# Block 0 of a fused attention and two-layer kernel: the third weight chunk's conversions placed behind the input's squares and its root, with 24 filler matmuls in place of 36

## The chip, the cores and the metric

The kernel runs on one core of a Trainium2 chip. The metric is device time in microseconds (us), the median of several runs. One more execution is recorded by the hardware profiler, and all rows of the trace come from that one.

## The reference

Attention over 4 batches, 8 heads, 576 positions of 64 numbers: the first four heads see a local window of 32 positions, the other four see every 32nd position. Its output, 2304 tokens of 512 numbers, goes through two gated layers with 1536 inner columns, the first behind a normalisation by the root of the mean square:

```
scores = where(mask, q @ k.T / 8, -1e9);  x = softmax(scores) @ v
rms = sqrt(mean(x * x) + 1e-6);  xn = x / rms * rms_g
y   = (silu(xn @ w_gate) * (xn @ w_val)) @ w_out
out = ((y @ w_a) * (y @ w_b)) @ w_out2
```

Every product keeps about single precision: both factors are split into a high part and a low part, and three matmuls (hi hi, hi lo, lo hi) are summed.

## The kernel before, in words

The 2304 tokens are worked through in 6 blocks of 384 (t = 0 to 5). In each block the attention's output gives four tiles of 128 x 384, the inputs 0 to 3. Inputs 0 and 1 come from the local heads, 2 and 3 from the strided ones. The first layer then runs over 12 chunks of 128 inner columns (fc). Per chunk PE makes a gate product g_ps and a value product v_ps of 12 matmuls each (`mm_in`, lines 485 to 488, `mm3`, 480 to 483), VectorE (DVE) multiplies g_ps by the reciprocal root `rinv` into sg (line 774), ScalarE (ACT) takes silu (776), DVE multiplies by v_ps (787), `split` makes the high part on ACT (506) and the low part (507), both called hl, and PE adds the 12 output matmuls (y) of the chunk before (`emit_y`, 595 to 603). The second layer follows after block 5. Three PSUM banks serve g_ps and v_ps in turn; in block 0 the product with sg is written over v_ps, so such a bank is held until hl is made.

Block 0 has more to do: the weights arrive as 64-bit words and are converted while it runs. A conversion (`conversion`, `words`, `parts`, lines 113 to 169) is one list of three steps: two activations on ACT (lines 137 and 142), an or-step on DVE (145); then the high part, a cast on ACT (150), and the low part, a subtraction on GpSimd, POOL (151). Gate and value weights of a chunk go together, 1024 columns (`convert1`, 543 to 550; chunk 0 in two halves), output weights alone, 512 columns (lines 789 to 793), and are then written out for the later blocks by a DMA on SP (793). SP also issues the loads (line 111).

The root's path in block 0: `xhl` (383 to 390) scales an input tile into its high part on ACT (387), squares it on ACT (432), and makes its low part on DVE (389). A matmul with a matrix of ones adds the squares of each of the four inputs (436). Two buffers hold squares, so the third square needs the first sum's matmul, the fourth the second's. `rinv` (446 to 450) is the square root on ACT (448) and the reciprocal on DVE (450). `keep_busy` (558 to 563) issues filler matmuls that nobody reads, 128 x 256 in bfloat16: 20 at the start (WARM) and 36 here, "id36" in STEPS0 (line 42), not before the last transpose of the inputs.

The order of instructions on each engine is chosen when the program is built, by a planner that has its own estimate of durations; once built, each engine runs its list in order. `behind` and `gate` (lines 496 to 502 and 581 to 587) bind that order: what is traced inside comes, on an engine, after the named instruction on the same engine. They add no wait between engines. `GATES` (line 45) lists for the chunks 0, 1, 2, 3 and from 4 on which instructions those are: "xhi" is the last scaled copy of an input (ACT), "sqrt" the root (ACT), "rec" the reciprocal (DVE), "snorm", "sqr" and "pvr" are steps of the strided attention on DVE, "pvm" one on POOL.

Of the kernel before, what the change touches and what calls it, by code (L numbers as in the profile page):

```python
# [14 lines left out]
AF = mybir.ActivationFunctionType  # L15
# [23 lines left out]
LOADS0 = "la0 lq ls0 cst la1 lb0 lvl1 lb1 lvl0 lv0"  # L39
STEPS0 = ("sqk00 sqk01 sqk02 qk0 qk1 qk2 smask0 lmax0 lexp0 smask1 lmax1 lexp1 smask2 ssub sexp "  # L40
          "lnorm0 snorm lmax2 lexp2 pt0 ptc0 lnorm1 sqrt_set pt1 ptc1 spv00 spv01 spv02 lnorm2 pt2 "
          "ptc2 pv0 pvc0 pv1 pvc1 xst0 xst1 xstc0 id36 xstc1 rms rinv")
WARM = 20

GATES = ["pvm snorm sqr",
         "norm pvm snorm sqr",
         "pvr snorm xhi",
         "snorm sqr sqrt xhi",
         "rec sexp snorm sqrt xhi"]

# [17 lines left out]
WLO = ["PPP", "PPP", "PPP", "PPP", "PPP", "PPP",  # L68
       "PPP", "PPP", "PPP", "PPP", "PPP", "PPD"]

LOW = ["AAA"] * NFC
# [6 lines left out]
def fused_kernel(ctx: ExitStack, tc: tile.TileContext, qtl, ktl, vl, qs, ks, vs, cst, w1, w2, out):  # L78
# [5 lines left out]
    nc = tc.nc  # L84

    def engine(c):
        return {"P": nc.gpsimd, "D": nc.vector}[c]
# [17 lines left out]
    def gv_slot(dtype, name):  # L105
        return wgt.tile([128, 2, 2, DM], dtype, tag="gv", name=name, bufs=NFC)
# [18 lines left out]
    def words(third, z, low="A"):  # L125

        third = third.rearrange("p a n -> p (a n)")
        raw = third.rearrange("p (n t) -> p n t", t=2)
        y = raw[:, :, 1].bitcast(F32)

        def first():
            nc.scalar.activation(y, y, AF.Prelu, scale=-2.0 ** -80, alpha=-2.0 ** -32)
            if low == "D":
                nc.vector.tensor_scalar(z(), raw[:, :, 0], 29, None, op0=ALU.logical_shift_right)
            else:  # L140
                half = third.bitcast(U16).rearrange("p (n t) -> p n t", t=4)[:, :, 1]
                nc.scalar.activation(z(), half, AF.Copy, scale=2.0 ** -13, bias=2.0 ** -14 - 0.5)

        def second():
            nc.vector.scalar_tensor_tensor(z(), raw[:, :, 1], 3, z(), op0=ALU.logical_shift_left, op1=ALU.bitwise_or)

        return [first, second]

    def parts(x, hi, lo, lo_eng):
        nc.scalar.copy(hi, x)  # L150
        lo_eng.tensor_tensor(lo, x, hi.bitcast(F32), op=ALU.subtract)  # L151

    def conversion(third, ready, pool, lo_eng, low, out=False):

        st = {}
        n = ready.shape[1] // 2

        def z():
            if not st:
                st["z"] = pool.tile([128, (1 if out else 2) * DM], U32, tag=f"cz{out}", name="cz", bufs=NCZ[out])  # L160
            return st["z"][:, :n * DM]

        def last():
            x = z().bitcast(F32).rearrange("p (a n) -> p a n", a=n)
            hl = ready.rearrange("p (a s) n -> p a s n", s=2)
            parts(x, hl[:, :, 0], hl[:, :, 1], lo_eng)

        return words(third, z, low=low) + [last]

    def run(steps):  # L170
        for f in steps:
            f()
# [14 lines left out]
    def attention(t, pool, psum, banks):  # L187
# [4 lines left out]
        st = {}  # L192
        steps = {}

        def bank():
            return psum.tile([128, 512], F32, tag=next(banks), name="att")

        def piece(tag, name, bufs):
            return pool.tile([128, NTB], F32, tag=tag, name=name, bufs=bufs)
# [228 lines left out]
        def sq(i):  # L428
            def f():
                q_t = st["sq", i] = piece("sq", "sq", 2)  # L430
                src = st["ops" if i < 2 else "xps", i % 2][:, :NTB]
                nc.scalar.activation(q_t, src, AF.Square)
                if t == 0:
                    if i == 0:
                        st["rps"] = bank()
                    nc.tensor.matmul(st["rps"][:, :NTB], ones, q_t, start=i == 0, stop=i == 3)
                elif i:
                    engine(SQA[t]).tensor_tensor(q_t, q_t, st["sq", i - 1], op=ALU.add)
            return f
# [54 lines left out]
    silu, silu_gate = [], []  # L494

    @contextmanager
    def behind(instructions):

        with ExitStack() as e:
            for i in instructions:  # L500
                e.enter_context(tc.issue_after(i))
            yield
# [21 lines left out]
    pool = apool.enter_context(tc.tile_pool(name="early", bufs=1))  # L524
# [18 lines left out]
    def convert1(fc):  # L543
        t = gv[fc] = gv_slot(F32R, "gv")
        two = [raw.pop((fc, k)) for k in range(2)]
        if fc in FUSEDW:
            both, ready = gvraw[fc], t.rearrange("p k a n -> p (k a) n")
            run(conversion(both.rearrange("p k a n -> p (k a) n"), ready, pool, engine(WLO[fc][0]), LOW[fc][0]))
        else:
            run(zipped(*(conversion(two[k], t[:, k], pool, engine(WLO[fc][k]), LOW[fc][k]) for k in range(2))))  # L550

# [16 lines left out]
    s0 = attention(0, pool, psum, itertools.cycle(["att", "y0", "y1", "y2", "y3"]))  # L568
# [12 lines left out]
    @contextmanager  # L581
    def gate(fc):

        with behind(silu[:1] if fc > 4 else []), ExitStack() as e:
            for key in GATES[min(fc, len(GATES) - 1)].split():
                e.enter_context(tc.issue_after(s0["st"][key].ins))
            yield

    with gate(0):
        convert1(0)  # L590
# [22 lines left out]
    def load_wo(t, fc):  # L613
        wt = wo[t, fc] = wo_tile()
        nc.sync.dma_start(wt.rearrange("p a n -> p (a n)").bitcast(F32), wod[fc])
# [126 lines left out]
    for t in range(NB):  # L742
        if t == 1:
            apool.close()
            pool = apool.enter_context(tc.tile_pool(name="attn", bufs=1))
        if t == NB - 1:
            apool.close()
            cpool.close()
            pool = p2.enter_context(tc.tile_pool(name="forms", bufs=1, reuse_waits="tile"))
            early = [f for k in (4, 5, 0, 1, 2, 3) for f in convert_forms(k, k < 4)]  # L750
        nxt = attention(t + 1, pool, psum, itertools.cycle(["att"])) if t + 1 < NB else None
        if t == 0:
            exps(nxt)
        x = [xt[t, cc] for cc in range(NCC)]
        for fc in range(NFC):
            if t > 0 and fc == 0:
                load_wo(t, 0)
            g_ps = psum.tile([128, 512], F32, tag="gv", name="g_ps", bufs=3)
            mm_in(g_ps[:, :NTB], gv[fc], 0, x)
            v_ps = psum.tile([128, 512], F32, tag="gv", name="v_ps", bufs=3)  # L760
            mm_in(v_ps[:, :NTB], gv[fc], 1, x)
            if t == 0 and fc + 1 < NFC:
                with gate(fc + 1):
                    convert1(fc + 1)
                if fc + 2 == NFC:
                    load_late([(NFC - 2, 2), (NFC - 1, 2)])
            if t == NB - 1:
                slab[fc] = wgt.tile([128, 4 * DM], F32 if fc in (0, 1, 11) else F32R, tag="gv", name="slab", bufs=NFC)
                with behind(made):
                    run(early[len(early) * fc // NFC:len(early) * (fc + 1) // NFC])  # L770
                    for k in [k for k in x0 if k <= fc]:
                        run(x0.pop(k))
            sg = tmp("sg")
            nc.vector.tensor_tensor(sg, g_ps[:, :NTB], ri[t], op=ALU.mult)  # L774
            with behind(silu_gate):
                silu.append(nc.scalar.activation(sg, sg, AF.Silu).ins)  # L776
            silu_gate[:] = []
            if fc == 1 and t > 0:
                evac_y(t - 1)
            if nxt is not None:  # L780
                attention_slot(nxt, fc)
            if prev is not None:
                emit_y(*prev)
            if t > 0 and fc + 1 < NFC:
                load_wo(t, fc + 1)
            h = tmp("h") if t else v_ps[:, :NTB]
            made[:] = [nc.vector.tensor_tensor(h, sg, v_ps[:, :NTB], op=ALU.mult).ins]
            hl[t, fc] = split(h, engine(HLO0[fc] if t == 0 else HLO[t]))
            if t == 0:
                wt = wo[0, fc] = wo_tile()  # L790
                with gate(fc + 1), behind(silu[:1] if fc > 1 else []):
                    run(conversion(raw.pop((fc, 2)), wt, pool, engine(WLO[fc][2]), LOW[fc][2], True))
                nc.sync.dma_start(wod[fc], wt.rearrange("p a n -> p (a n)").bitcast(F32))
                if fc % 2 and units:
                    load_units(1)
            prev = (t, fc)
# [140 lines left out]
    steps = [(ps, g, p) for ps in (range(0, 3), range(3, 6)) for g in range(NB // 2) for p in ps]  # L937
# [3 lines left out]
    for i, (ps, g, p) in enumerate(steps):  # L941
# [12 lines left out]
        a, pa = products(g, 2 * p)  # L954
# [82 lines left out]
```

## Time and profile before

| | us |
|---|---|
| median of 3 runs | 964.89 |
| lowest and highest of them | 964.42, 965.96 |
| the profiled execution | 967.4 |
| its span in the trace | 965.6 |
| mean granted PE clock in it | 0.985 of full speed |

The span is what the trace shows from the first to the last instruction; the profiled execution's own time has 1.8 us more around it, and it is 2.51 us above the median. All positions below are us from the span's start. In a row of a timeline the columns are start, duration, engine, line, operation, output<-input, shape, count, and in brackets the idle time of the engine before it and who ended it. PEld is PE's loading of weights. A row with a count covers that many instructions, merged.

### The profile page before, as it was taken

Reading aid. Unit: us, or ns where it says so; the run is one execution under the profiler, and the core shown is the slowest. Engines: PE = TensorE matmul, PEld = TensorE weight load, DVE = VectorE, ACT = ScalarE, POOL = GpSimd, SP = SyncE. Lnnn points to the kernel's source line nnn. Section 1 sums busy time; section 2 is a strip of 40 time slices with the busy share of each in tenths; the row PEclk is TensorE's granted clock in tenths of the full one; section 3 lists DMA queues with packets and bytes.
Section 4 is the critical chain, followed back from the end, with each engine's and each line's share of the span. In section 5 each row is a group of like instructions: output and inputs, shape, how many; then the busy total and the mean of one; then the engine's idle time right before and its main releaser. Section 6 shows DMA issues by size and latency. Waiting matters only on the chain.

```text
span 965.6 us, 14099 instructions
## 1 busy us (share of the span) xinstructions
PE 937.1 (97%) x5318; PEld 888.2 (92%) x5318; DVE 621.5 (64%) x900; ACT 425.3 (44%) x795; POOL 539.5 (56%) x407
## 2 busy tenths in 40 slices
PE   5998999999999999999999899999999999999998
PEld 4898999999999999999999898899999998999996
DVE  5658858658819895986666378658655655564534
ACT  5988646344433434434555455436425422122110
POOL 3567946558649677878479545655724423123211
PEclk6899999999999999999999999999999999999999
DMA  9974286537535563532788884996993974754701
GB/s 342 408 262 151 89 288 218 151 96 225 165 104 161 161 204 102 185 105 87 284 324 306 329 306 166 402 415 247 385 373 114 345 274 165 284 205 168 267 2 66
DMA packets 57363, 215.55 MB, mean 223 GB/s; under 512 B 5968, under 2 KB 14544, under 8 KB 51664
## 3 DMA queue, kind: packets, MB, share of 16 engines
q1 hardware_dynamic: 57296, 214.66, 61.3%
q8 instruction: 42, 0.69, 0.3%
q14 instruction: 25, 0.20, 0.1%
HBM read 172.17 MB, written 42.47 MB: 222 GB/s over the span
## 4 chain that ended last, share of the span: by engine, by line
PE 65%; DMA 11%; DVE 7%; POOL 7%; ACT 4%; issue 4%; SPq 0%; DVEq 0%; ACTq 0%; POOLq 0%
PE o L916 5%; PE o L918 5%; PE o L917 5%; DMA raw<-in_w 4%; POOL prod L248 4%; PE Y L862 4%; PE Y L861 4%; PE Y L860 4%; DMA gv_raw<-in_w 3%; PE y L482 3%; PE y L481 3%; PE g_ps L483 3%; PE y L483 3%; PE g_ps L482 3%; PE g_ps L481 3%
## 5 line engine op out<-in xcount | busy, mean ns | idle before, releaser
L151 POOL TENSOR_TENSOR hl<-c,hl 128x384 fp32r<-128x384 f32 x72 | 77.9, 1082 | 181.0 <-ACT hl L150 174.4
L248 POOL TENSOR_TENSOR prod<-kv_t,qs_t 128x512 f32<-128x512 f32 (+12 forms) x57 | 108.3, 1921 | 15.3 <-DMA kv_t<-in_ks 8.2
L481 PE MATMUL v_ps<-xx,gv 128*128 128x384 f32 x288 | 97.7, 339 | 1.9 <-DVE sg L774 1.8
L482 PE MATMUL y<-hl,wo 128*128 128x384 f32 x288 | 98.1, 341 | 1.1 <-POOL hl L507 1.1
L281 POOL TENSOR_TENSOR prod<-kv_t,S_t 128x512 f32<-128x512 f32 (+12 forms) x57 | 86.2, 1526 | 21.1 <-issue 7.1
L482 PE MATMUL v_ps<-xx,gv 128*128 128x384 f32 x288 | 97.9, 340 | 0.0
L483 PE MATMUL v_ps<-xx,gv 128*128 128x384 f32 x288 | 97.8, 340 | 0.0
L481 PE MATMUL g_ps<-xx,gv 128*128 128x384 f32 x288 | 97.5, 339 | 0.0
L483 PE MATMUL g_ps<-xx,gv 128*128 128x384 f32 x288 | 97.3, 338 | 0.0
L482 PE MATMUL g_ps<-xx,gv 128*128 128x384 f32 x288 | 96.9, 337 | 0.0
L867 DVE TENSOR_TENSOR c<-c,Y 128x384 f32<-128x384 f32 x108 | 59.0, 551 | 58.8 <-PE Y L862 53.5
L507 POOL TENSOR_TENSOR hl<-h,hl 128x384 fp32r<-128x384 f32 x60 | 64.1, 1069 | 58.4 <-ACT hl L506 57.3
L483 PE MATMUL y<-hl,wo 128*128 128x384 f32 x288 | 95.0, 338 | 0.0
L284 DVE TENSOR_REDUCE xs_t<-prod 128x64 f32<-128x448 f32 (+17 forms) x57 | 85.7, 1521 | 9.7 <-POOL prod L281 9.5
L481 PE MATMUL y<-hl,wo 128*128 128x384 f32 x288 | 85.0, 343 | 7.0 <-ACT hl L506 5.4
L916 PE MATMUL o<-slab,hl 128*128 128x512 f32 x216 | 84.7, 393 | 1.8 <-DVE slab L925 1.3
L917 PE MATMUL o<-slab,hl 128*128 128x512 f32 x216 | 84.5, 392 | 0.0
L918 PE MATMUL o<-slab,hl 128*128 128x512 f32 x216 | 83.2, 394 | 0.0
L150 ACT CAST hl<-c 128x384 fp32r<-128x384 f32 x72 | 37.0, 514 | 93.8 <-DVE c L897 93.5
L776 ACT ACTIVATE sg<-sg 128x384 f32<-128x384 f32 x72 | 38.0, 528 | 86.4 <-DVE sg L774 86.0
L862 PE MATMUL Y<-slab,form 128*128 128x384 f32 x216 | 73.0, 338 | 0.0
L861 PE MATMUL Y<-slab,form 128*128 128x384 f32 x216 | 73.0, 338 | 0.0
(137 smaller groups left out, 2491.4 us busy)
## 6 DMA issues: line engine op xcount, KB each, us to landing
form<-formd SPq DMA_DIRECT2D x32, 1792.0 KB, 10.7
wo<-wod SPq DMA_DIRECT2D x60, 512.0 KB, 3.8
raw<-in_w SPq DMA_DIRECT2D x40, 512.0 KB, 7.3
gv_raw<-in_w SPq DMA_DIRECT2D x32, 512.0 KB, 10.2
formd<-form SPq DMA_DIRECT2D x6, 1792.0 KB, 7.5
formd<-forms SPq DMA_DIRECT2D x6, 1792.0 KB, 12.8
slab<-x2d SPq DMA_DIRECT2D x24, 384.0 KB, 4.0
wod<-wo SPq DMA_DIRECT2D x12, 512.0 KB, 3.4
```

Source lines behind the costliest of these rows:

```text
L151: lo_eng.tensor_tensor(lo, x, hi.bitcast(F32), op=ALU.subtract)
L248: nc.gpsimd.tensor_tensor(pr, st["ks", g][:, :, :n, :], st["qs"][:, heads(g), mm:mm + 1, :].to_broadcast([128, G, n, D]), op=ALU.mult)
L281: st["pvm"] = nc.gpsimd.tensor_tensor(pr, st["vs", g][:, :, :n, :], st["S"][:, heads(g), mm, :n, None].to_broadcast([128, G, n, D]), op=AL ...
L284: st["pvr"] = nc.vector.tensor_reduce(st["xs"][:, mm, heads(g), :], pr.rearrange("p g n d -> p g d n"), axis=X, op=ALU.add)
L481: nc.tensor.matmul(out_ps, w_hi, x_hi, start=start, stop=False)
L482: nc.tensor.matmul(out_ps, w_hi, x_lo, start=False, stop=False)
L483: nc.tensor.matmul(out_ps, w_lo, x_hi, start=False, stop=stop)
L861: nc.tensor.matmul(bank(n), hi, x[p][:, 1, c], start=False, stop=False, skip_group_check=not begins)
L862: nc.tensor.matmul(bank(n), lo, x[p][:, 0, c], start=False, stop=c == 1, skip_group_check=not begins)
L916: nc.tensor.matmul(o, h[:, 0, cols], w[0], start=n == 0, stop=False)
L917: nc.tensor.matmul(o, h[:, 0, cols], w[1], start=False, stop=False)
L918: nc.tensor.matmul(o, h[:, 1, cols], w[0], start=False, stop=n == len(chunks) - 1)
```

## The change

In `GATES`, the entry for chunk 2 gets "square" (the last square, on ACT) and "xlo" (the last low part of an input, on DVE). In `convert1` the last step of chunk 2's conversion (cast and low part) is put behind the root. The output weights of chunk 1, which used the entry of chunk 2, use that of chunk 3, whose member on ACT is the root. The fillers are 24.

```diff
-          "ptc2 pv0 pvc0 pv1 pvc1 xst0 xst1 xstc0 id36 xstc1 rms rinv")
+          "ptc2 pv0 pvc0 pv1 pvc1 xst0 xst1 xstc0 id24 xstc1 rms rinv")
...
-         "pvr snorm xhi",
+         "pvr snorm xhi square xlo",
...
-                nc.scalar.activation(q_t, src, AF.Square)
+                st["square"] = nc.scalar.activation(q_t, src, AF.Square)
...
-            run(conversion(both.rearrange("p k a n -> p (k a) n"), ready, pool, engine(WLO[fc][0]), LOW[fc][0]))
+            steps = conversion(both.rearrange("p k a n -> p (k a) n"), ready, pool, engine(WLO[fc][0]), LOW[fc][0])
+            run(steps[:-1])
+            with behind([s0["st"]["sqrt"].ins] if fc == 2 else []):
+                run(steps[-1:])
...
-                with gate(fc + 1), behind(silu[:1] if fc > 1 else []):
+                with gate(3 if fc == 1 else fc + 1), behind(silu[:1] if fc > 1 else []):
```

## Rows read from the trace of the kernel before

**Rows 1.** The page: engine, busy us, share of the span, instructions.
```profile
PE 937.1 (97%) x5318; PEld 888.2 (92%) x5318; DVE 621.5 (64%) x900; ACT 425.3 (44%) x795; POOL 539.5 (56%) x407
```
**Rows 2.** Stretches of the head: busy us of each engine, granted PE clock, DMA share, GB/s.
```profile
29.00:30.00 1.00, 1.00 (x10) 0.85 (x9) 0.67 (x2) 0.83 (x1) 0.00 (x0) 0.87 1.03 397
...
33.70:49.95 16.25, 14.62 (x79) 13.13 (x76) 10.82 (x13) 15.92 (x23) 6.51 (x3) 1.00 1.03 408
49.95:51.80 1.85, 0.02 (x1) 0.02 (x1) 0.10 (x2) 1.85 (x4) 1.37 (x1) 1.00 1.06 415
51.80:58.00 6.20, 6.20 (x26) 6.20 (x27) 3.40 (x5) 6.20 (x10) 2.25 (x2) 0.72 1.04 400
...
86.30:94.20 7.90, 4.90 (x19) 4.35 (x20) 7.84 (x13) 7.87 (x14) 2.84 (x2) 0.78 0.68 239
```
**Rows 3.** Timeline of PE, fillers to the first gate matmul.
```profile
27.87 2.59 PE L563 MATMUL idle<-ones 128*128 128x256 bf16 x16
...
30.95 0.93 PE L563 MATMUL idle<-ones 128*128 128x256 bf16 x7
31.71 0.81 PE L436 MATMUL att<-sq,ones 128*128 128x384 f32 x2
32.36 1.58 PE L563 MATMUL idle<-ones 128*128 128x256 bf16 x13
33.70 0.42 PE L481 MATMUL g_ps<-xx,gv 128*128 128x384 f32 x1
```
**Rows 4.** Timeline of ACT, chunk 2's first activation to the cast of hl 0.
```profile
31.90 1.16 ACT L137 ACTIVATE gv_raw<-gv_raw 128x1024 f32<-128x1024 f32 x1
...
35.05 0.92 ACT L432 ACTIVATE sq<-att 128x384 f32<-128x384 f32 x2
...
37.72 0.58 ACT L448 ACTIVATE rms_t<-att,eps_sb 128x384 f32<-128x384 f32 x1 [0.30 <-PE att L436]
...
49.28 1.07 ACT L150 CAST gv<-cz 128x1024 fp32r<-128x1024 f32 x1
...
51.23 0.50 ACT L506 CAST hl<-v_ps 128x384 fp32r<-128x384 f32 x1
```
**Rows 5.** Timeline of DVE, chunk 1's or-step to chunk 4's.
```profile
26.80 2.34 DVE L145 SCALAR_TENSOR_TENSOR cz<-gv_raw,cz 128x1024 uint32<-128x1024 uint32 x1 [1.30 <-ACT cz L142]
...
34.10 1.83 DVE L145 SCALAR_TENSOR_TENSOR cz<-gv_raw,cz 128x1024 uint32<-128x1024 uint32 x2 [2.37 <-ACT cz L142]
35.85 1.13 DVE L389 SCALAR_TENSOR_TENSOR xx<-att,cst_sb,xx 128x384 fp32r<-128x384 f32 x2
38.34 2.55 DVE L450 RECIPROCAL rinv<-rms_t 128x384 f32<-128x384 f32 x1 [1.35 <-ACT rms_t L448]
40.81 1.16 DVE L145 SCALAR_TENSOR_TENSOR cz<-gv_raw,cz 128x1024 uint32<-128x1024 uint32 x1
41.89 1.01 DVE L774 TENSOR_TENSOR sg<-g_ps,rinv 128x384 f32<-128x384 f32 x2
42.81 1.22 DVE L145 SCALAR_TENSOR_TENSOR cz<-gv_raw,cz 128x1024 uint32<-128x1024 uint32 x1
```
**Rows 6.** Timeline of PE, its waits for sg 0 and hl 0.
```profile
42.48 0.45 PE L481 MATMUL v_ps<-xx,gv 128*128 128x384 f32 x1 [0.96 <-DVE sg L774]
...
51.78 0.97 PE L481 MATMUL y<-hl,wo 128*128 128x384 f32 x4 [1.85 <-ACT hl L506]
```
**Rows 7.** Timeline of POOL: chunk 0's output weights, and chunk 7's low part.
```profile
26.79 1.26 POOL L151 TENSOR_TENSOR wo<-cz,wo 128x512 fp32r<-128x512 f32 x1
...
79.65 2.86 POOL L151 TENSOR_TENSOR gv<-cz,gv 128x1024 fp32r<-128x1024 f32 x1
```
**Rows 8.** Timeline of PE: first gate matmul of chunk 7.
```profile
84.05 0.33 PE L481 MATMUL g_ps<-xx,gv 128*128 128x384 f32 x1
```
**Rows 9.** SP's timeline, the first weight loads; and the tile gv_raw's loads.
```profile
8.82 25.92 SPq L111 DMA_DIRECT2D gv_raw<-in_w  x24
...
DMA to landing us min/median/max: 3.5/10.2/10.9
```

## The prediction

> **What bounds the kernel now.** I read the page's busy times first: TensorE (PE) is busy 97% of the span [rows 1]. So a change pays only where PE idles, runs at the lower of its clock levels, or does work nobody needs, and what it saves early reaches the end only if no later wait gives it back. I then cut the head into stretches [rows 2]. In 33.70 to 49.95 us PE is busy 14.62 of 16.25 us, ScalarE (ACT) 15.92: ACT is the engine without slack there. In the next 1.85 us PE does nothing. In 51.80 to 58.00 it is busy throughout at a mean granted clock of 0.72; if x of the stretch ran at half, 1 - 0.5x = 0.72, x = 0.56, so 3.5 us at 1.2 GHz and 1.7 us lost. The same pair, idling and then a lower clock, stands at 86.30 to 94.20.
>
> The timelines give the order. PE runs 16, 7 and 13 fillers, with the sums of squares of inputs 0 and 1 between them, and starts the first gate matmul at 33.70 [rows 3]. ACT takes chunk 2's conversion at 31.90, ahead of the last two squares at 35.05, and the root starts at 37.72 [rows 4]. VectorE (DVE) likewise converts at 34.10 and makes the last two lo parts only at 35.85; the reciprocal runs 38.34 to 40.89, chunk 3's conversion to 41.97, and then come sg of chunks 0 and 1 [rows 5]. PE waits 0.96 us for sg at 42.48, and 1.85 us for hl of chunk 0, whose cast is at 51.23 on ACT [rows 4, 6]. That cast's input has been ready since soon after silu; ACT has just taken other conversions first. Those don't wait for data: the 24 weight loads are issued by 8.82 + 25.92 = 34.74 and none takes over 10.9 us, so all have landed by 45.6 [rows 9].
>
> **Part 1, 12 fillers fewer.** The last 13 took from 32.36 to 33.70, 0.103 us each [rows 3]; 12 are 1.24 us. They are on PE's path if the first gate matmul's inputs are there sooner, and they are: input 1's lo part precedes the 2.37 us of DVE idling in front of 34.10, hence is done by 31.73 [rows 5]. Cover that goes: the fillers kept PE active. The clock rises in 29 to 30 us [rows 2], before the 24th filler, and real matmuls follow at once, so I cost the loss of cover at nothing; bound: if PE had to go back to half clock for as long as in [rows 2], +1.7 us.
>
> **Part 2, conversions behind squares and lo parts.** The second sum of squares starts at 31.71 and lasts 0.81 [rows 3], to 32.52, and frees the buffer for the last square, which takes half of the pair's 0.92 us [rows 4]: squares done at about 33.0 against 35.97. ACT idles up to 0.5 us for it, which I charge in that figure. The lo parts move from 36.98 to about 33, where DVE is idle now [rows 5]; Nothing of this part is on the queues of SP or POOL. From squares to root start was 37.72 - 35.97 = 1.75, so the root could start at 34.75; ACT will be inside chunk 2's two activations (33.0 + 2 x 1.16 = 35.3 at most [rows 4]; spans of neighbours overlap by some 0.1). I take 35.1, **2.6 us earlier**; bounds 1.5 (one more activation of 1.16 ahead) and 3.0. Reciprocal, sg 0, silu 0 and h 0 hang on it in turn. PE's 0.96 us wait goes: with the fillers gone it reaches that matmul at 42.48 - 0.96 - 1.24 = 40.3, and sg 0, half of the pair's 1.01, then ends by 41.89 + 0.5 - 2.6 = 39.8 [rows 5, 6]. So PE is through chunk 2 at 49.95 - 1.24 - 0.96 = 47.75.
>
> **Part 3, chunk 2's cast and chunk 1's output weights behind the root.** This takes a cast of 1024 columns (1.07, as at 49.28 [rows 4]) and two activations and a cast of 512 (an estimate: half of 1.16 each, 1.7) from before the root to after it: 2.8 us of ACT work, no longer ahead of the root. No work is added, and ACT's total up to the cast of hl 0 stays. Here I choose. Between root and that cast ACT spends 51.23 - 37.72 = 13.51 us [rows 4]. If the planner puts the cast the same time behind the root, as its chain of inputs suggests, the cast moves with the root by 2.6 us, and 2.6 us of later conversions fall behind it; if ACT's order up to the cast stays whole, it moves by nothing. I take 2.6; ends 0 and 3.0. The output weights' lo part on POOL and their write on SP come later by some 3 us; POOL has the room (idle before chunk 2's lo part), and chunk 1's output weights are not used before chunk 0's.
>
> What becomes late next: chunk 2's lo part. Its or-step waits for the reciprocal or goes just before it, so cast at 38.5 to 39.5 and lo part 2.4 us more, 42 at the latest; PE wants chunk 2 at 44.6 - 2.2 = 42.4 (42.48 plus 12 matmuls of 14.62 / 79 = 0.18 each [rows 2, 6], less the head start). It just holds.
>
> **Sum at the first output matmul:** 51.78 - 2.6 = 49.2 us, with PE idling 49.2 - 47.75 = 1.45 instead of 1.85. Gain 2.6, and because idling stays near what it was I take the later clock fall as unchanged.
>
> **How much is kept.** Chunk 7's lo part ends on POOL at 79.65 + 2.86 = 82.51 and is first read by the third gate matmul after 84.05, at 84.4 [rows 7, 8]: 1.9 us of slack if its chain doesn't move. It partly hangs on PE itself (next block's scores), so 1.9 to 2.6; I take the middle, **2.3 us**. The profiled execution took 967.4 us (span 965.6), so 965.1; the median of the runs is 964.89, 2.5 under the profiled one, so I forecast 964.89 - 2.3 = **962.6**. What a measurement of this kernel can tell from no change is 0.2%, 1.9 us: the edges are 962.96 and 966.82. The forecast lies just past the first. Its own range is 961.0 (hl 0 moved 3.0 and some of the wait at 86.30 gone) to 963.5 (root only 1.5 earlier).
>
> **Rivals.**
> *The clock holds as well.* If PE's idling at the first output matmul shrinks to well under 1.85 us, the half clock of 51.80 to 58.00 may not come: 1.7 us more on top of 2.6, giving 960.6. For it: two of three idle spells shrink. Against: 1.45 us remain by my sum. Range to 959.3, if hl 0 also comes 1.3 us earlier.
>
> *Order stays, gain is swallowed.* ACT is saturated, and if the planner leaves the cast of hl 0 behind the same list, the first output matmul stays at 51.78 and PE idles 4.0 us instead of 1.85 there. 964.9, the old time. For it: ACT's 15.92 of 16.25. The change would then do what it says (root early) and move no end.
>
> *VectorE beside GpSimd.* The or-step L145 of 1024 columns took 2.34 us while POOL was subtracting (POOL until 28.05) and 1.16 us at 40.81 [rows 5, 7]. Chunk 2's lo part now falls on chunk 3's or-step, 1.1 us more on DVE ahead of h 0: gain 2.3 - 1.1 = 1.2, 963.7. The Trainium skill, GPSIMD Engine Reference, section 1 (Specifications), says the two share their SBUF interface and contend when VectorE reads two SBUF inputs, as L145 does; by that rule the slow row is no accident, and the trace's pair of durations agrees.
>
> *Slower: chunk 2 comes late.* Its cast now waits for the root and takes its place in ACT's queue. Chunk 4's or-step ended at 44.03 and its cast ran at 49.28: 5.25 us queued [rows 4, 5]. The same for chunk 2 gives cast at 39.4 + 5.25 = 44.65, lo part from 45.7 to 48.1. PE, at chunk 2 by 42.4, would idle over 5 us in one piece. It decides at 46.8: from the third matmul of chunk 2 to the first output matmul are 22 matmuls of 0.18 and a wait for sg of about 0.96, 5.0 us, and 51.78 - 5.0 = 46.8. Ending at 48.1 costs 1.3, and a second fall of the clock 1.7 [rows 2]: +3.0, **967.9**. Against it: squares, sums and root leave ACT nothing else that may run before the root than chunk 2's activations, so its cast is next in line.
>
> **Chances.** Forecast 0.36 (0.24 of it past the edge, 0.12 short of it), clock holds 0.19, swallowed 0.17, VectorE beside GpSimd 0.08, chunk 2 late 0.20 (0.19 past 966.82). Of the swallowed case 0.02 comes out faster and 0.03 slower, since the rest of block 0 is planned anew and its waits are uncosted. Faster 0.24 + 0.19 + 0.02 = 0.45; slower 0.19 + 0.03 = 0.22; same the remaining 0.33. The range runs from 959.3 to 967.4: it takes in all but the half of the slow case that is above it.
>
> **What would show it.** Right: squares on ACT straight behind the last scaled copy, root near 35, no wait for sg at the second value matmul, cast of hl 0 near 48.6, first output matmul near 49. Swallowed: root early, yet first output matmul at 51 to 52 with a 4 us wait. Late: PE waiting for gv of chunk 2 from about 42. Clock: the granted clock at 1.00 through 58. Wrong altogether: root not earlier than 37, or PE waiting for inputs ahead of 33.

## The result, and the profile after

The changed kernel took 972.80 us (median of 4 runs, 971.07 to 973.31) against 965.42 us beside it: a ratio of 1.0069, 95% interval 1.0055 to 1.0083. It is **slower by 0.7%**, where 962.6 was forecast and 959.3 to 967.4 was the range. The profiled execution took 972.63 us with a span of 970.9; the span before was 965.6, so the rows below have 5.3 us to explain. (The medians lie 7.4 us apart; the profiled execution before was itself 2.51 us above its median.)

The page after, then stretches of the head (columns as in [rows 2]):

```profile
PE 936.7 (96%) x5306; PEld 887.1 (91%) x5306; DVE 624.4 (64%) x900; ACT 425.1 (44%) x795; POOL 539.2 (56%) x407
```
```profile
33.70:49.95 16.25, 13.30 (x63) 12.13 (x62) 9.83 (x9) 13.84 (x19) 3.82 (x2) 0.89 1.03 408
42.40:46.10 3.70, 3.69 (x13) 3.69 (x14) 2.97 (x3) 3.67 (x5) 1.42 (x1) 0.56 1.02 407
49.95:54.55 4.60, 1.47 (x10) 1.15 (x8) 1.98 (x3) 4.60 (x8) 3.29 (x2) 1.00 1.06 402
```

PE is about as busy as before (936.7 against 937.1 us), so the time went into idling. In 33.70 to 49.95 both PE (13.30, before 14.62) and ACT (13.84, before 15.92 [rows 2]) do less. The timelines of PE, ACT and DVE after:

```profile
32.26 0.42 PE L481 MATMUL g_ps<-xx,gv 128*128 128x384 f32 x1
...
34.78 0.81 PE L436 MATMUL att<-sq,ones 128*128 128x384 f32 x2
...
36.50 0.81 PE L436 MATMUL att<-sq,ones 128*128 128x384 f32 x2
...
42.41 0.44 PE L481 MATMUL v_ps<-xx,gv 128*128 128x384 f32 x1 [2.30 <-DVE sg L777]
...
54.55 0.97 PE L481 MATMUL y<-hl,wo 128*128 128x384 f32 x4 [3.13 <-ACT hl L506]
```
```profile
31.70 0.51 ACT L432 ACTIVATE sq<-att 128x384 f32<-128x384 f32 x1
32.44 0.49 ACT L432 ACTIVATE sq<-att 128x384 f32<-128x384 f32 x1 [0.23 <-PE att L436]
...
37.34 0.58 ACT L448 ACTIVATE rms_t<-att,eps_sb 128x384 f32<-128x384 f32 x1 [2.38 <-PE att L436]
...
54.04 0.46 ACT L506 CAST hl<-v_ps 128x384 fp32r<-128x384 f32 x1
...
62.22 2.00 ACT L150 CAST gv<-cz 128x1024 fp32r<-128x1024 f32 x2 [0.31 <-DVE cz L145]
```
```profile
37.96 2.55 DVE L450 RECIPROCAL rinv<-rms_t 128x384 f32<-128x384 f32 x1 [1.74 <-ACT rms_t L448]
40.43 1.46 DVE L145 SCALAR_TENSOR_TENSOR cz<-gv_raw,cz 128x512 uint32<-128x512 uint32 x1
41.81 1.01 DVE L777 TENSOR_TENSOR sg<-g_ps,rinv 128x384 f32<-128x384 f32 x2
```

The squares are done at 32.93, where the prediction had 33.0. But the last two sums stand in PE's list behind gate and value matmuls of chunk 0: the third sum behind 14 of them, at 34.78, the fourth behind 6 more, at 36.50. The root comes at 37.34, 0.38 us earlier than before [rows 4]; of that, 0.18 us stand already at the fillers, which begin at 27.69 against 27.87 [rows 3]. In the kernel before the same 14 matmuls stood ahead of both sums, and these ran in one piece (a sum is two records):

```profile
36.23 1.45 PE L436 MATMUL att<-sq,ones 128*128 128x384 f32 x4
```

ACT has nothing to do until then: the change forbids it the casts. It idles 2.38 us. DVE takes an or-step of output weights between reciprocal and sg, and sg 0 is where it was (41.81 against 41.89 [rows 5]). That or-step of 512 columns took 1.46 us, with POOL making chunk 2's low part up to 41.34; in the kernel before, one of 512 columns took 0.69 us with POOL idle. So some 0.8 us of what sg 0 waits for is this meeting. First POOL after, then DVE before:

```profile
38.94 2.40 POOL L151 TENSOR_TENSOR gv<-cz,gv 128x1024 fp32r<-128x1024 f32 x1 [6.47 <-ACT gv L150]
```
```profile
46.34 0.69 DVE L145 SCALAR_TENSOR_TENSOR cz<-gv_raw,cz 128x512 uint32<-128x512 uint32 x1 [0.55 <-ACT cz L142]
```

PE, 1.44 us ahead (the fillers and that 0.18), waits 2.30 us for sg 0 and then runs at a granted clock of 0.56 in 42.40 to 46.10, so near the lower level for most of it. The first output matmul comes at 54.55, 2.8 us later than in [rows 6], behind a wait of 3.13 us. Behind this wait, the longer one, the clock stayed at 1.00:

```profile
54.55:60.00 5.45, 5.45 (x31) 5.45 (x32) 2.99 (x5) 5.45 (x10) 3.04 (x2) 1.00 0.69 274
```

The evacuation of block 0's output, before and after, and three of PE's later waits after:

```profile
136.41 1.94 DVE L610 TENSOR_TENSOR ys<-y,rinv 128x384 f32<-128x384 f32 x4
```
```profile
142.75 1.95 DVE L613 TENSOR_TENSOR ys<-y,rinv 128x384 f32<-128x384 f32 x4 [0.74 <-PE y L483]
```
```profile
88.65 0.44 PE L481 MATMUL g_ps<-xx,gv 128*128 128x384 f32 x1 [2.04 <-DVE sg L777]
...
105.35 0.98 PE L483 MATMUL y<-hl,wo 128*128 128x384 f32 x4 [1.16 <-POOL wo L151]
...
137.74 0.44 PE L481 MATMUL g_ps<-xx,gv 128*128 128x384 f32 x1 [2.25 <-DVE sg L777]
```

Block 0 ends 6.3 us later (its evacuation starts at 142.75 against 136.41), of which 2.8 stand at the first output matmul; behind block 0 nothing more is lost (5.3 at the span's end). So there are two losses to explain: one in the head, one in the rest of block 0.

### The profile page after: what moved, and what is told of

It reads as the page before. It is cut to its first block, busy times and chain, and to the rows that moved or that the text cites. A ratio compares the mean times of both kernels' runs of the same rounds, so it can differ in the third digit from the quotient of the medians.

```text
span 970.9 us, 14076 instructions
## 1 busy us (share of the span) xinstructions
PE 936.7 (96%) x5306; PEld 887.1 (91%) x5306; DVE 624.4 (64%) x900; ACT 425.1 (44%) x795; POOL 539.2 (56%) x407
## 4 chain that ended last, share of the span: by engine, by line
PE 70%; POOL 8%; DVE 6%; DMA 5%; ACT 5%; issue 4%; SPq 0%; DVEq 0%; POOLq 0%; ACTq 0%
PE o L919 5%; PE o L921 5%; PE o L920 5%; POOL prod L248 5%; PE Y L865 4%; PE Y L864 4%; PE Y L863 4%; DMA raw<-in_w 3%; PE g_ps L483 3%; PE g_ps L481 3%; PE y L482 3%; PE g_ps L482 3%; PE y L481 3%; PE y L483 3%; PE v_ps L481 3%
## 5 line engine op out<-in xcount | busy, mean ns | idle before, releaser
L481 PE MATMUL g_ps<-xx,gv 128*128 128x384 f32 x288 | 97.6, 339 | 4.3 <-DVE sg L777 4.3
L481 PE MATMUL v_ps<-xx,gv 128*128 128x384 f32 x288 | 97.4, 338 | 2.9 <-DVE sg L777 2.9
L481 PE MATMUL y<-hl,wo 128*128 128x384 f32 x288 | 85.5, 345 | 6.6 <-ACT hl L506 3.1
L150 ACT CAST hl<-c 128x384 fp32r<-128x384 f32 x72 | 37.0, 514 | 94.0 <-DVE c L900 93.8
```

The costliest lines, as they stand in the source:

```text
L481: nc.tensor.matmul(out_ps, w_hi, x_hi, start=start, stop=False)
```

## Experiments: the parts of the change, each planned anew

Theories at first. A: the casts put behind the root leave ACT idle. B: the missing fillers. C: the squares' place. And against all three: any edit makes the planner write another order for all of block 0. Every ratio here is to the kernel before, run beside it on the same chip; four runs of this round shared a median of 966.68.

**fill24**, the kernel before with 24 fillers and nothing else:

```diff
-... xst1 xstc0 id36 xstc1 rms rinv")
+... xst1 xstc0 id24 xstc1 rms rinv")
```

> Kernel before with 24 fillers alone. Theory A (ScalarE idles before the root because the conversions were put behind it): ScalarE keeps chunk 2's and chunk 1's conversions ahead of the root here, idles under 0.5 us in front of it, and the time stays within 0.3% of before (962.5 to 968.3 us). Theory B (the 12 fillers were useful, or their loss alone re-plans the block badly): 0.5% to 0.8% slower than before, 970 to 973 us, with the wait for sg 0 at about 2.3 us.

Measured: 970.58, ratio 1.0046 (1.0034 to 1.0058), with ACT not idling from 30 us to its root at 37.97, and PE waiting 2.18 us for sg 0. These are theory B's numbers; which of its two readings holds, p_fill24 below decides. **after36**, the change with 36 fillers again:

> Changed kernel with 36 fillers. Theory A: ScalarE still idles about 2 us before the root, cast of hl 0 stays near 54, time at least 970 us. Theory B: back to before, 963 to 968 us.

Measured: 971.04, 1.0054 (1.0041 to 1.0068); ACT idles 1.89 us before the root, as theory A has it. **gate24**, before with 24 fillers and the first of the change's edits alone:

```diff
-         "pvr snorm xhi",
+         "pvr snorm xhi square xlo",
```

> Only the entry of chunk 2 (behind the last square and the last low part) and 24 fillers; cast and output weights may run before the root. Theory A: ScalarE fills the time to the root with them, idles under 0.7 us, cast of hl 0 at 52 or earlier, time 962 to 968 us. Theory B: as the changed kernel, 970 to 973 us. Theory C (squares ahead of conversions are themselves the harm): also 970 to 973 us, but with ScalarE busy before the root.

Measured: 970.07, 1.0043 (1.0027 to 1.0060). The head did what theory A wanted (ACT idle 0.17 us before the root, cast of hl 0 at 51.32), and the time missed A's range and fell in that of B and C; p_early below, with the squares first and the order held, speaks against C. **sumfirst**, the change with chunk 0's matmuls behind the last sum:

```diff
-            mm_in(g_ps[:, :NTB], gv[fc], 0, x)
+            with behind([s0["st"]["sum"].ins] if (t, fc) == (0, 0) else []):
+                mm_in(g_ps[:, :NTB], gv[fc], 0, x)
```

> Changed kernel with chunk 0's gate and value matmuls bound behind the last sum of squares on TensorE. If what failed is that the sums sit behind 14 to 20 gate and value matmuls on TensorE, the root moves from 37.3 to 34.5 to 35.2, ScalarE's idle time before it falls from 2.4 to under 1.0 us, and the cast of hl 0 comes at 52 or earlier: at least 2 us faster than the changed kernel, under 971. If the planner's later order decides instead, the root moves as said and the time stays at 971 to 974.

Measured: 969.26, 1.0027 (1.0017 to 1.0037), under 971 as the first reading has it. Two of its rows, from ACT and PE:

```profile
34.52 0.60 ACT L448 ACTIVATE rms_t<-att,eps_sb 128x384 f32<-128x384 f32 x1
```
```profile
48.61 0.96 PE L481 MATMUL y<-hl,wo 128*128 128x384 f32 x4 [0.60 <-ACT hl L506]
```

Here the head does what the prediction wanted: root 3.2 us and first output matmul 3.2 us earlier than before (0.3 us of each stand already at the fillers), and still the kernel is slower. None of the parts tried alone was harmless; giving the fillers back repaired little (after36), and putting the sums first repaired more than half (1.0027 against 1.0069). What all four share is a newly planned order, and this calls for runs in which the order is held.

## Experiments: the same edits with the order held

For these, each engine's instructions are chained in a list that the kernel carries; the chain orders an engine's own list and adds no wait between engines. What follows are edits of that list, and lines stand 28 further down than in the kernel before (L150 is L178, L481 is L509).

```diff
+def keep_order(tc):
...
+        for a, b in zip(chain, chain[1:]):
+            tc.add_manual_dep(b, a.name, dep, reason="plan")
```

**p_fill24**, before's order with twelve fillers struck out:

> The kernel before with 24 fillers in place of 36, and every engine's order of work in the whole kernel bound to that of the kernel before, so that nothing is planned anew. Theory order: the twelve fillers lie under the wait for the root, the first gate matmul comes 1.24 us earlier and the wait for sg 0 grows from 0.96 to about 2 us, first output matmul at 51.6 to 51.8, time 964.5 to 967.5 (no change). Theory fillers: they were worth something themselves (the clock falls in the longer wait, as in the run with 24 fillers and a free order): 969 to 971.

Measured: 964.81, ratio 0.9986 (0.9977 to 0.9995), in the range of theory order; the wait for sg 0 was 1.23 us and not 2, since PE waited 0.57 us for a square as well. The fillers cost nothing to remove; if anything 0.14% is gained, less than the 0.2% that the prediction gave as what a measurement can tell. So fill24's 0.46% is the re-planned order. **p_head**, the changed kernel's order up to the first output matmul, before's behind it:

> The order of the changed kernel on every engine up to the first output matmul (its 24 fillers, squares ahead of the conversions, casts behind the root), the order of the kernel before in all that follows. Theory both parts: the head is worth its own 2.8 us at the first output matmul, the later order the other 2.5 to 3.5: 968 to 969.5 here. Theory head alone: the late start and the fall of the clock at 43 us make all of it: 971 to 973. Theory later order alone: what the head loses is caught up by less waiting later: 965.5 to 967.

Measured: 967.91, 1.0022 (1.0013 to 1.0031). **p_tail**, the other way round:

> The order of the kernel before up to the first output matmul (36 fillers), the order of the changed kernel in all that follows. Theory both parts: 968.5 to 970, with first output matmul at 51.8 and block 0's output sums evacuated about 3 us later than in the kernel before. Theory head alone: 965.5 to 967. Theory later order alone: 970.5 to 973.

Measured: 971.32, 1.0049 (1.0036 to 1.0062). The two parts add up: 0.22% and 0.49% make 0.71%, and the change costs 0.69%. So the theory of both parts holds, with the later order the larger part. By the ranges in us it was less clear: p_head came out 0.1 us under the range of that theory, and p_tail 1.3 us over it, inside the range of "later order alone". That the later order is not the whole is shown by p_head's interval, which lies above 1. Against p_fill24, which has the same 24 fillers, p_head is 0.36% slower. p_tail's waits of PE in the later stretch are the changed kernel's, but for one of 0.15 us; the three of them shown above:

```profile
85.75 0.44 PE L509 MATMUL g_ps<-xx,gv 128*128 128x384 f32 x1 [2.01 <-DVE sg L802]
...
102.48 0.97 PE L511 MATMUL y<-hl,wo 128*128 128x384 f32 x4 [1.15 <-POOL wo L179]
...
134.96 0.45 PE L509 MATMUL g_ps<-xx,gv 128*128 128x384 f32 x1 [2.33 <-DVE sg L802]
```

Behind the first output matmul, up to the end of block 0, PE waits nine times in p_tail, 9.0 us in sum; in the kernel before four times, 4.4 us (0.71 + 2.13 + 0.16 + 1.39). The 4.6 us between them are about p_tail's loss (971.32 - 965.75 = 5.6 by the medians, 4.7 by the ratio). Which of the moves in that order makes each wait was not tried one by one.

**p_early**, an order by hand, to see what an early root is worth when little else is moved:

> An order written out by hand: the kernel before with 24 fillers; squares of the last two quarters and their lo parts ahead of the third chunk's conversion, the last two sums right behind the 24th filler, the root behind gv 2's two preparing steps, and silu 0, silu 1, the casts of h 0 and h 1 pulled ahead of the weight conversions of later chunks; all the rest in the order of the kernel before. Theory order: root at 34.5, sg 0 at 39, first output matmul at 46 to 47 with no wait ahead of it, 5 us earlier than before; of these 2 to 5 us are kept, 960.5 to 964. Theory conversions: the rest of block 0 is bound by the weight conversions of ScalarE, VectorE and GpSimd, whatever the head does, and the gain goes into waits for them: 965 to 968.

Measured: 965.75, 1.0001 (0.9992 to 1.0010). The root came at 33.95, the first output matmul at 46.14, 5.6 us earlier than before (0.8 us of it stand already at the fillers) and without a wait, PE's clock stayed at 1.00 to 62, and none of it was kept: theory conversions, by its time. In its stretch table ACT is busy 32.07 of 33 us from 29 to 62, as in the kernel before (32.11). The last two casts of that backlog, gv of chunks 5 and 6, with p_fill24's, p_idle's and p_head's (p_idle is the next run):

```profile
59.44 2.02 ACT L178 CAST gv<-cz 128x1024 fp32r<-128x1024 f32 x2
```
```profile
58.99 1.98 ACT L178 CAST gv<-cz 128x1024 fp32r<-128x1024 f32 x2
```
```profile
62.50 1.98 ACT L178 CAST gv<-cz 128x1024 fp32r<-128x1024 f32 x2
```
```profile
62.53 2.00 ACT L178 CAST gv<-cz 128x1024 fp32r<-128x1024 f32 x2 [0.60 <-DVE cz L173]
```

The early head brings these casts no sooner (59.44 against 58.99); a head in which ACT idles 2.2 us before its root, as p_head's does, moves them by 3.5. In the changed kernel they start at 62.22, in the one before at 59.58.

## Experiments: what the backlog is worth, and where the gain stops

**p_idle** tests that with another head in which the root comes earlier but ACT idles:

> The kernel before with 24 fillers and its order bound, but for two places of the head: on ScalarE the squares right behind the third chunk's two preparing steps and wo 1's two steps and both casts behind the root, so that ScalarE idles until the sums are done; on VectorE the lo parts and the reciprocal ahead of wo 1's or-step. Theory ScalarE's backlog: TensorE gets sg 0 about 1 us sooner, but ScalarE idles some 2 us before the root, the casts of gv 5 and gv 6 at the end of its full stretch come some 2 us later than with the order of before, and the time is 1.2 to 2.5 us over that of 24 fillers in the order of before (964.8): 966 to 967.3. Theory first output matmul: only when hl 0 is ready counts, which comes no later here: 964 to 965.5.

Measured: 969.12, 1.0026 (1.0017 to 1.0036). ACT idled 1.84 us ahead of its root at 36.41, and behind it twice more, for or-steps of DVE:

```profile
42.10 0.62 ACT L178 CAST wo<-cz 128x512 fp32r<-128x512 f32 x1 [1.01 <-DVE cz L173]
...
45.20 1.05 ACT L178 CAST gv<-cz 128x1024 fp32r<-128x1024 f32 x1 [0.39 <-DVE cz L173]
```

That makes 3.24 us. The casts slipped by 3.5 us, more than the 2 expected, and against p_fill24 the time rose by 0.40%, 3.9 us, past both ranges. ACT's idle time, the slip of its casts and the loss in time are of one size here, and not far apart in p_head (2.16 and 0.60 us idle, 3.5 us, 0.36% or 3.5 us against p_fill24). On which way the delay goes on from ACT is not shown: sg 0 came no sooner than in p_fill24 (42.59 against 42.07), and the first output matmul, which hangs on ACT's cast of hl 0, slipped as far as the casts of gv (54.64, and 54.29 in p_head, against 51.15 in p_fill24). The part of theory A that was wrong is only that it was the whole.

**p_late** and **p_pull** work on ACT's list elsewhere, **p_best** joins them to p_early's head:

> The kernel before with 24 fillers and its order bound, and two instructions of ScalarE moved around 80 to 90 us: the copy of pt 0 ahead of the eight exponentials, and the cast of hl that the output matmul at 88 us waits for ahead of one weight step. Theory order: the waits of 1.22 and 2.11 us there are made by ScalarE's order alone and shrink to some 0 to 1 us each: 962 to 964. Theory conversions: another engine's work stands behind those waits, and the time stays at 964.3 to 965.5.

> The kernel before with 24 fillers and its order bound, and on ScalarE the first steps of six output weights that are not wanted yet put behind the conversions of gv 5 and gv 6. Theory ScalarE's backlog: the casts of gv 5 and gv 6 start at 54.5 to 56 us instead of 59, GpSimd's long stretch starts as much sooner, and of that 1 to 3 us reach the end where nothing else holds: 962 to 964. Rival: with the head of before TensorE is not waiting for these casts at all, nothing is gained: 964.3 to 965.5.

> The early head of the run before last with both later edits: squares and root first, silu and hl casts ahead of later weights, the six output weights' first steps behind gv 5 and gv 6, the copy of pt 0 and the cast of hl moved forward at 80 to 90 us. Theory ScalarE's backlog: with the backlog moved the early head's 5 us are no longer eaten at 62 us, 960 to 963. Theory of a later floor: attention's own chain for the next block (exponentials, normalizing, copies) sets 85 us whatever comes before: 963.5 to 965.5.

Measured: p_late 966.86, 1.0006 (0.9997 to 1.0015); p_pull 965.30, 0.9987 (0.9978 to 0.9996); p_best 966.78, 1.0004 (0.9995 to 1.0013). p_pull came out as its rival says; p_late and p_best lie above all ranges that were written down for them. In p_pull the first of the two casts came 2.7 us earlier (56.29) and the time stayed p_fill24's. So in these runs the backlog costs when it is late and pays nothing when early. In p_late the wait of 1.22 us vanished, the other grew from 2.11 to 4.00, and DVE shows why. First p_fill24's two steps, then p_late's:

```profile
82.87 0.53 DVE L374 TENSOR_SCALAR lsm<-lsm 64x8 f32<-64x8 f32 x1 [2.37 <-ACT s_t L364]
...
83.67 1.49 DVE L376 TENSOR_TENSOR s_t<-s_t,lrs 64x512 f32<-64x512 f32 x1
```
```profile
83.33 1.29 DVE L374 TENSOR_SCALAR lsm<-lsm 64x8 f32<-64x8 f32 x1 [2.85 <-ACT s_t L364]
...
84.89 2.56 DVE L376 TENSOR_TENSOR s_t<-s_t,lrs 64x512 f32<-64x512 f32 x1
```

The two steps began 0.46 us later and lasted 1.83 us longer, with h, which the output matmul waits for, queued behind them.

Two pairs then mended one wait after the other, each with the late and the early head. First ACT's order at 79 to 88 us (**p_pullexp**, **p_allexp**), then also sg ahead of an or-step on DVE (**p_pullsg**, **p_allsg**):

> The run with six output weights' first steps put off, and in addition, on ScalarE around 79 to 88 us, the eight exponentials ahead of two weight casts, and the copy of pt 0 and the cast of hl right behind silu. Theory ScalarE's order in front of the output matmul at 88 us: exponentials at 79.0 instead of 80.06, hl cast near 85 instead of 87.5, that output matmul at 85.5 to 86.5, time 962.5 to 964.3. Theory contention: VectorE's steps of the exponentials' sums fall beside other work of GpSimd, take over 1 us more, and the matmul comes at 87.5 to 88.5: 964.8 to 966.5.

> The early head, the six output weights' first steps put off, and the same order of ScalarE around 79 to 88 us as in the other run of this pair. Theory ScalarE's order: if the floor at 88 us is ScalarE's order there, the early head shows no more than the late one (the exponentials wait for VectorE and the scores), both 962.5 to 964.3. Theory early head: TensorE's lead of some 4 us at 62 us is kept beyond 88 us once that order is mended: 960.5 to 962.5. Theory contention: 964.8 to 966.5.

> The late head with six weights put off and ScalarE's order mended at 79 to 88 us, and in addition, on VectorE, the sg that TensorE waited 3.54 us for put ahead of a weight step, with hl's lo part behind it. Theory order: that wait shrinks to under 1 us, TensorE runs on from 85 us, time 962 to 964.3. Theory of another floor: the next thing that TensorE wants there (scores' transposes, hl of the chunk after) is as late, and the time stays at 964.5 to 966.8.

> The same with the early head. Theory order: as the run beside it or better, 960.5 to 964.3; if it is better by 1 us or more, part of the early head's gain is kept. Theory of another floor: 964.5 to 966.8, equal to the run beside it within its interval.

Measured, in this order: 966.57, 1.0004 (0.9995 to 1.0013); 966.78, 1.0008 (0.9999 to 1.0017); 965.66, 0.9996 (0.9987 to 1.0006); 965.48, 0.9992 (0.9983 to 1.0001). The first pair's times lie 0.1 and 0.3 us above the range of contention, the second pair's in that of another floor. The output matmul did come at about 85, as the first pair expected, and PE then waited 3.54 and 4.12 us for sg; with sg first, the wait moved on, to the next transposes (1.40 at 89.76) and to output weights (1.35 at 102.12). Early and late heads are equal within their intervals. No version beat the plain p_fill24 or p_pull, the two whose intervals lie below 1, by 0.14% and 0.13%.

What all of these meet again is the last conversion of output weights and the next block's root behind it. ACT's rows for that step's second activation in p_fill24, p_early, p_allsg, p_idle and p_head:

```profile
125.09 0.67 ACT L170 ACTIVATE cz<-raw 128x512 uint32<-128x512 uint16 x1 [1.40 <-POOL wo L179]
```
```profile
124.55 0.66 ACT L170 ACTIVATE cz<-raw 128x512 uint32<-128x512 uint16 x1 [1.40 <-POOL wo L179]
```
```profile
125.45 0.67 ACT L170 ACTIVATE cz<-raw 128x512 uint32<-128x512 uint16 x1 [1.39 <-POOL wo L179]
```
```profile
128.82 0.67 ACT L170 ACTIVATE cz<-raw 128x512 uint32<-128x512 uint16 x1 [1.40 <-POOL wo L179]
```
```profile
128.76 0.67 ACT L170 ACTIVATE cz<-raw 128x512 uint32<-128x512 uint16 x1 [1.39 <-POOL wo L179]
```

The step before it waits 0.41 to 0.52 us for the load of its raw weights in these five runs, and the root, silu and the last output matmul of the block follow. With before's later order, the nine runs whose casts of gv 5 and gv 6 did not slip have this step between 124.55 and 126.33, the kernel before at 126.11; the two whose casts slipped have it 3.7 us after p_fill24's. The profile's chain of the work that ended last suggests why a lead of PE is not kept. In p_fill24 it runs through PE from the first output matmul to the next block's scores; in p_early it leaves PE and runs over conversions on DVE, a load of weights and POOL, and is back at PE only at 75.61. Three pieces of each, p_fill24 first:

```profile
51.15 0.97 PE y L509 x4
62.35 0.86 PE att L324 x8
72.98 1.08 PE att L324 x16
```
```profile
54.32 1.24 DVE cz L173
55.58 5.04 DMA gv_raw<-in_w
60.61 2.38 POOL gv L179
```

That fits chains of nearly one length that lie side by side: where one is shortened, or two as in p_best and in the early runs of the last pairs, the next one holds. This, and that the chain at 125 us bounds the block, is a reading of these rows; a run that shortens that chain itself was not made.

## Why the prediction was wrong, step by step

**Part 1, the fillers: right, and worth some 0.14% by themselves.** The first gate matmul moved by 1.44 us (1.24 forecast, and 0.18 stand already at the fillers), and the loss of cover was rightly costed at nothing in itself (p_fill24, 0.9986). But in the changed kernel the 1.24 us were carried into "PE is through chunk 2 at 47.75", which leaned on part 2: with sg 0 where it was, they became wait, 0.96 to 2.30 us.

**Part 2, the first step that failed: "From squares to root start was 37.72 - 35.97 = 1.75, so the root could start at 34.75".** The 1.75 us were not a property of the squares. Between them and the root stand two sums on PE, in PE's own list. In the kernel before, 14 matmuls of chunk 0 stood ahead of both sums, so that the sums began only at 36.23, and then took 1.45 us; the new list keeps these 14 and puts 6 more between the sums. The root gained 0.38 us, not 2.6. sumfirst shows that the step was repairable: with the sums first, root at 34.52, 0.2 us beyond the early bound of 37.72 - 3.0.

**Part 3: "No work is added, and ACT's total up to the cast of hl 0 stays".** The total stayed but for one activation of 512 columns; the idle time did not: casts that had filled ACT's wait for the sums were moved behind it, and 2.38 us of an engine with 0.33 us of slack in 16.25 [rows 2] were thrown away. That is the size of the head's loss (p_head, 0.22% or 2.1 us, with ACT idle 2.16 us; p_idle is a second such head). The prediction had named ACT as "the engine without slack there", and then priced up to 0.5 us of idling ahead of the last square and none between the squares and the root. Its choice that the cast of hl 0 moves with the root ("I take 2.6; ends 0 and 3.0") failed too: the planner put it at 54.04, 2.81 us later, and the ends didn't include a loss.

**How much is kept: "1.9 to 2.6; I take the middle, 2.3 us", the step with the largest price.** It asked only whether chunk 7's lo part would still be in time. In sumfirst and p_early the gain at the first output matmul was really there, and the time rose by 0.27% and by nothing. The term should have been bounded below by zero or less: the whole block is planned anew, and that alone cost 0.49% in p_tail, of the change's 0.69%, and 0.46% in fill24. The prediction gave this, "its waits are uncosted", 0.03 of chance. Which moves of the new order make its waits stays open.

**The rivals.** None named what happened. "Swallowed" came nearest, with a wait at the first output matmul grown to 3.13 us, but by another way (the root wasn't early). "Chunk 2 comes late" had the right sign and engine and a wrong place: chunk 2's gate matmuls follow without a wait. "VectorE beside GpSimd" was real, and close to its place: chunk 2's low part fell on DVE's or-step ahead of sg 0, though on that of the output weights, and took some 0.8 us there (1.46 against 0.69). "The clock holds as well" had its sign met, 1.00 from 51.80 to 58.00, without its gain and against its reason, since PE's wait there had grown to 3.13 us. "Wrong altogether: root not earlier than 37" is the sign that was given and met.

## What to carry to other kernels

Where an engine is saturated, an instruction put behind a later event costs the idle time it used to fill; ask of each moved piece what runs in its old place. Follow a chain through the in-order lists of every engine that it crosses: the squares were early, and two sums in another engine's list, behind 20 of its matmuls, kept the root nearly where it was. And before an edit of an order is timed, hold the rest of the order fixed: of this change's 0.7%, 0.5% was the planner's new order far behind the edit, and a clean part (12 fillers) measured +0.46% with the order free and -0.14% with it held.

## What the runs showed of the hardware

Two of DVE's steps, L374 and L376, waited for the end of the POOL instruction that was running. In p_late L374 on 64 x 8 elements ends at 84.62 and POOL's subtraction of output weights at 84.59; the L376 behind it ends at 87.45, and POOL's next subtraction at 86.90, 0.55 us before. In p_fill24 the pairs are 83.40 with 83.38, and 85.16 with 84.61. In p_pullexp POOL idled when L376 came, and it took 0.68 us instead of 1.49 or 2.56. POOL's rows of p_fill24 and p_late, and p_pullexp's L376:

```profile
81.54 1.84 POOL L276 TENSOR_TENSOR prod<-kv_t,qs_t 128x768 f32<-128x768 f32 x1
83.34 1.27 POOL L179 TENSOR_TENSOR wo<-cz,wo 128x512 fp32r<-128x512 f32 x1
```
```profile
83.32 1.27 POOL L179 TENSOR_TENSOR wo<-cz,wo 128x512 fp32r<-128x512 f32 x1
84.56 2.34 POOL L179 TENSOR_TENSOR gv<-cz,gv 128x1024 fp32r<-128x1024 f32 x1
```
```profile
83.37 0.68 DVE L376 TENSOR_TENSOR s_t<-s_t,lrs 64x512 f32<-64x512 f32 x1
```

So the price of such a meeting is, in these rows, not a rate but the rest of the other engine's instruction. Not every step of DVE pays it: sg, which reads one factor from PSUM, took 0.56 us at 79.94 in p_fill24, while POOL subtracted from 77.93 to 80.79, and 0.54 us at 88.54 with POOL idle. The Trainium skill, GPSIMD Engine Reference, section 1 (Specifications), names contention for VectorE instructions in a two-port mode or with two SBUF inputs; L376 with its two inputs agrees, and so does sg with one of its two in PSUM. L374 has one tensor as input; on 64 x 8 it took 0.16 us at 160.47 in p_fill24 with POOL idle, and 0.53, 1.29 and 1.45 us beside POOL in p_fill24, p_late and p_pullexp. In which mode it ran no run here shows.

The granted clock fell behind some of PE's waits and not behind others as long: to 0.72 behind 1.85 us [rows 2] and 0.56 behind 2.30 us (42.40 to 46.10 after), but it stayed at 1.00 behind 3.13 us (54.55 to 60.00 after) and behind 2.71 us in gate24 (42.50 to 46.50). In sumfirst and p_early, whose heads have no wait over 0.7 us, it stayed at 1.00 to 62 us, and neither was faster than the kernel before.
